# Retention and expert kernel: the block's output turned back by transposes, with the gate logits taken from the turned-over side in four column groups and added up over the heads by one product

## The chip, the cores and the metric

The kernel runs on one core of one Trainium2 chip. The metric is the device time of one execution in microseconds (us); of several executions the median is given. The profile is one execution on the same core, taken by the hardware profiler. Engines are named as in its rows: PE is TensorE's matmuls and PEld its weight loads, DVE is VectorE, ACT is ScalarE, POOL is GpSimd, SP is SyncE, which issues most transfers.

## The reference

A retention layer (attention with a decay per head, no softmax) over 4 batches of 768 tokens with 8 heads of 64, then a layer of 8 experts of which each token takes one:

```python
gamma = 1.0 - 2.0 ** (-5.0 - np.arange(H, dtype=np.float32))
scale = 1.0 / np.sqrt(D)
for t in range(S):
    state = gamma[None, :, None, None] * state + np.einsum('bhd,bhe->bhde', k[:, :, t], v[:, :, t])
    y[:, :, t] = scale * np.einsum('bhd,bhde->bhe', q[:, :, t], state)
...
x = np.ascontiguousarray(attn_out.transpose(0, 2, 1, 3)).reshape(B * S, H * D)
...
logits = x @ w_gate + modality_bias[modality_id]
e_idx = np.argmax(logits, axis=1)
...
h = np.maximum(x[mask] @ w1[e], 0.0)
out[mask] = gate_w[mask, None] * (h @ w2[e])
```

There are 3072 tokens; `x` has 512 columns, an expert's inner layer 1024. `gate_w` is the softmax probability of the chosen expert. All is float32.

## The kernel before, in words

**Retention** goes through 24 blocks of 128 tokens, six to a batch. Of each block the kernel computes masked scores (PE, then DVE writes `a`, L212 in later blocks and L283 in earlier ones), the running state (`st`) and the block's output turned over, `yT`: features on the partitions, tokens along the row, four groups of 128 features, each group two heads. The decay is pulled apart: keys and values are scaled beforehand by a power that falls with the token's place, and the outputs have to be multiplied by `gain`, a number for each token and head. Blocks 0 to 8 are computed whole (`whole_scores`, `whole_state`, `whole_out`), blocks 9 to 23 in quarters, so that two small products run side by side in the array.

**`tokens_out(n, yT)`** (L367 to L406) makes rows of tokens out of `yT`. `wgt` holds for each of the four feature groups an identity of 128 columns (copied by DVE at L146) and beside it the gate's weights of that group's two heads, 16 columns. One product with `yT` as stationary operand and `wgt` as moving operand gives 144 columns: the group's features turned back, and the logits that each head adds, before the gain. Two groups go to one PSUM bank, two to another (`x_0`, `x_1`; four products, eight records, L375). DVE multiplies the logits of a bank by the gain (`lh`, L383), and the features of the first bank too (`xs`, L383); ScalarE does the features of the second bank, a head at a time (`xs`, four ACTIVATE, L397); at the end DVE adds up `lh` over the heads into `lg` (L404). The rows `xs` are later scattered to a table in DRAM, from which the experts fetch them; `lg` of three blocks goes through a routing step (softmax, choice, ranks, lists) in small pieces on all engines.

**Experts** work in jobs of 256 tokens. Weights come as `raw` by SP's queue; ScalarE takes the rounded part `hi_e` (L780), DVE the rest `lo_e` (L782); rows fetched are turned over by PE (`xp_e`, L825); first layer `h_e` (L840) and second layer `o_e` (L855) are products in three terms (hi hi, hi lo, lo hi). Late in the kernel the last tokens are done in units of 32 (`uh_u`, L909, a product in four column groups).

**Order.** The order on PE, ACT, DVE and SP is that in which the program's text issues the instructions (`tc.manual_schedule`). The retention is a generator. At first it runs alone, with the first expert weights fetched beside it; from about 67 us on it is mixed with the expert jobs: a job yields after each feature group, every third of its steps takes one step of the retention, every second one calls `tick()`, which takes the next routing piece from the list `todo`. `tokens_out` of a block is called after the step in which the next block's scores are masked. Thus between a block's `x` on PE and its `lh` on DVE there may stand masked scores, cuts of weights or routing pieces in DVE's queue, while PE has expert products behind `x` in its own.

## Time and profile before

| | |
|---|---|
| median of 3 runs | 431.44 us (429.03 to 433.25) |
| the profiled execution's own time | 433.4 us |
| its span, first to last instruction | 431.5 us, mean granted clock 0.978 |
| busy: PE, PEld | 403.3, 353.1 us |
| busy: DVE, ACT, POOL | 249.4, 207.6, 103.9 us |
| transfers | 92.79 MB, 215 GB/s in the mean |
| PE `x` (L375) | 192 records, 31.8 us, 24 blocks |
| DVE `lh` (L383), 128x32 | 48 instructions, 184 ns each |
| DVE `xs` (L383), 128x256 | 24 instructions, 414 ns each |
| DVE sum into `lg` (L404) | 24 instructions, 272 ns each |
| ACT `xs` (L397), 128x64 | 96 instructions, 315 ns each |

A row of the profile's groups gives line, engine, operation, the tile written and those read, the shapes, how many, then busy us and the mean of one in ns, then the idle time of the engine just before and what ended it. A row of the timeline gives start and duration in us, then engine, line, operation and tiles; in brackets the idle time before it and what ended that. A stretch is a window of time, with each engine's busy time in it, the clock granted to TensorE (1.00 is full), the share of time in which transfers ran, and GB/s. A row of the chain of waits gives start, duration and group; the chain is followed back from the last instruction. L12 is line 12 of the kernel.

### The profile page before, as it was taken

The page shows a single profiled execution, that of the slowest core. Times are in us where ns is not written, and L with a number is a line of the kernel's source. Part 1 is how long each engine was busy: PE and PEld are TensorE (multiplying, and loading weights), DVE is VectorE, ACT ScalarE, POOL GpSimd, SP SyncE. Part 2 cuts the span into 40 slices and gives each one's busy share as a digit, 9 for nine tenths or more (in the row PEclk, how much of TensorE's full clock was granted, in tenths as well). Part 3 has the DMA queues.
Part 4 walks back from the last instruction along what each step waited for, and adds up shares of the span by engine and source line. Part 5 has one row for each costly group of instructions (what it writes and reads, how often), then busy time and mean ns, then how long its engine had stood idle before and what let it go on. Part 6 is the DMA issues. An engine that isn't in the chain of part 4 may idle for free.

```text
span 431.5 us, 12024 instructions
## 1 busy us (share of the span) xinstructions
PE 403.3 (93%) x4596; PEld 353.1 (82%) x4596; DVE 249.4 (58%) x590; ACT 207.6 (48%) x420; POOL 103.9 (24%) x130
## 2 busy tenths in 40 slices
PE   4987979899999999999999999999999999999990
PEld 3876869888988977988888988979898998869850
DVE  1766547856636666646945765967564655635400
ACT  1324245635546455546545646636464646535310
POOL 2425301413052123113500401210774101001010
PEclk9999688999999999999999999999999999999997
DMA  8999746967796954237840304842264989995000
GB/s 287 388 402 333 306 165 235 356 203 238 238 349 244 323 212 154 88 103 235 281 162 27 139 21 160 254 162 75 94 226 125 367 286 350 352 394 219 2 25 20
DMA packets 30891, 92.79 MB, mean 215 GB/s; under 512 B 5550, under 2 KB 5678, under 8 KB 30832
## 3 DMA queue, kind: packets, MB, share of 16 engines
q1 hardware_dynamic: 25360, 77.83, 52.0%
q0 software_dynamic: 5184, 13.67, 8.7%
q8 instruction: 37, 0.61, 0.6%
q10 hardware_dynamic: 288, 0.50, 0.4%
q14 instruction: 22, 0.18, 0.1%
HBM read 94.84 MB, written 17.21 MB: 260 GB/s over the span
## 4 chain that ended last, share of the span: by engine, by line
PE 66%; issue 8%; DMA 5%; DVE 3%; ACT 2%; POOL 1%; POOLq 0%; SPq 0%; ACTq 0%
PE o_e L855 25%; PE h_e L840 23%; PE x L375 4%; PE st L267 3%; PE h_s L840 3%; PE sc L267 3%; PE y L267 2%; DMA wa_u<-in_w_dram 2%; PE xp_e L825 2%; DMA wb_u<-in_w_dram 2%; DMA kv<-in_qkv_dram 1%; DVE lo_e L782 1%; ACT hi_e L780 1%; ACT xs L397 1%; POOL out_dram L868 1%
## 5 line engine op out<-in xcount | busy, mean ns | idle before, releaser
L782 DVE TENSOR_TENSOR lo_e<-raw,hi_e 128x1024 fp32r<-128x1024 f32 x80 | 100.0, 1250 | 76.5 <-ACT hi_e L780 68.6
L840 PE MATMUL h_e<-xTh,hi_e 128*128 128x256 f32 x320 | 92.0, 287 | 0.0
L840 PE MATMUL h_e<-xTl,hi_e 128*128 128x256 f32 x320 | 90.3, 282 | 0.0
L840 PE MATMUL h_e<-xTh,lo_e 128*128 128x256 f32 x320 | 90.3, 282 | 0.0
L780 ACT CAST hi_e<-raw 128x1024 fp32r<-128x1024 f32 x80 | 83.8, 1049 | 2.8 <-DMA raw<-in_w_dram 2.8
L855 PE MATMUL o_e<-hi_e,hTh 128*128 128x512 f32 x160 | 66.1, 413 | 0.0
L855 PE MATMUL o_e<-lo_e,hTh 128*128 128x512 f32 x160 | 63.1, 395 | 0.0
L855 PE MATMUL o_e<-hi_e,hTl 128*128 128x512 f32 x160 | 63.1, 394 | 0.0
L840 PEld LDWEIGHTS h_e<-xTh,hi_e 128*128 128x128 f32 x320 | 60.9, 190 | 0.7
L840 PEld LDWEIGHTS h_e<-xTh,lo_e 128*128 128x128 f32 x320 | 60.7, 190 | 0.3
L840 PEld LDWEIGHTS h_e<-xTl,hi_e 128*128 128x128 f32 x320 | 60.8, 190 | 0.0
L868 POOL DMA_INDIRECT out_dram<-o_e,xg_e x20 | 21.5, 1073 | 109.7 <-ACT o_e L867 89.5
L789 ACT ACTIVATE hTh<-h_e 128x256 fp32r<-128x256 f32 x80 | 30.7, 388 | 33.7 <-PE h_e L840 29.9
L1024 POOL TENSOR_TENSOR vd<-kv,cst 128x512 f32<-128x512 f32 x24 | 26.5, 1103 | 74.7 <-DMA kv<-in_qkv_dram 29.9
L397 ACT ACTIVATE xs<-x,cst 128x64 f32<-128x64 f32 x96 | 22.3, 315 | 45.2 <-DVE lh L383 20.4
L481 POOL DMA_INDIRECT x_dram<-xs,pos x24 | 27.6, 1152 | 65.4 <-DVE a L212 29.8
L790 DVE SCALAR_TENSOR_TENSOR hTl<-h_e,hTh 128x256 fp32r<-128x256 f32 x80 | 33.0, 419 | 16.0 <-ACT hTh L789 14.4
L855 PEld LDWEIGHTS o_e<-lo_e,hTh 128*128 128x128 f32 x160 | 30.1, 188 | 7.1
L855 PEld LDWEIGHTS o_e<-hi_e,hTh 128*128 128x128 f32 x160 | 30.1, 188 | 6.2
L855 PEld LDWEIGHTS o_e<-hi_e,hTl 128*128 128x128 f32 x160 | 30.2, 189 | 5.6
L262 ACT COPY s<-st 128x256 f32<-128x256 f32 x36 | 13.6, 378 | 40.4 <-PE y L267 16.1
L867 ACT ACTIVATE o_e<-o_e,xg_e 128x512 f32<-128x512 f32 x20 | 13.8, 690 | 39.6 <-issue 24.0
(193 smaller groups left out, 696.0 us busy)
## 6 DMA issues: line engine op xcount, KB each, us to landing
raw<-in_w_dram SPq DMA_DIRECT2D x104, 512.0 KB
kv<-in_qkv_dram SPq DMA_DIRECT2D x24, 512.0 KB
kq<-in_qkv_dram SPq DMA_DIRECT2D x23, 512.0 KB
xg_e<-x_dram SPq DMA_DIRECT2D x20, 257.0 KB
wa_u<-in_w_dram SPq DMA_DIRECT2D x8, 512.0 KB
wb_u<-in_w_dram SPq DMA_DIRECT2D x16, 256.0 KB
xg_s<-x_dram SPq DMA_DIRECT2D x4, 257.0 KB
x_dram<-xs,pos POOLq DMA_INDIRECT x24
```

The source lines that it names most:

```text
L267: nc.tensor.matmul(out_, l, r, start=start, stop=True, skip_group_check=True)
L375: nc.tensor.matmul(px[:, g], yT[:, 2 * u + g], wgt[:, 2 * u + g], start=(g == 0), stop=(g == 1), skip_group_check=True,)
L397: nc.scalar.activation(x[:, i], px[:, i // 2, rows(i % 2)], AF.Copy, scale=gain[:, c, 4 * u + i : 4 * u + i + 1],)
L481: ins = nc.gpsimd.indirect_dma_start(out=x_dram[:, :], out_offset=bass.IndirectOffsetOnAxis(ap=pos[:, i : i + 1], axis=0), in_=xs, in_offs ...
L780: nc.scalar.copy(hi, raws[m][i])
L782: nc.vector.tensor_tensor(lo, raws[m][i], hi.bitcast(F32), op=ALU.subtract)
L789: nc.scalar.activation(hi, src, AF.Relu)
L790: nc.vector.scalar_tensor_tensor(lo, src, 0.0, hi.bitcast(F32), op0=ALU.max, op1=ALU.subtract)
L840: nc.tensor.matmul(ph, s["w1"][f // 2][wi][:, o : o + P], s["xT"][kc // 2][a][:, kc % 2, :], start=(n == 0), stop=(n == 3 * KC - 1),)
L855: nc.tensor.matmul(po, hT[f][a][:, hh * P : (hh + 1) * P], s["w2"][f // 2][wi][:, (f % 2) * DM : (f % 2 + 1) * DM], start=(n == 0), stop=( ...
L868: ins = nc.gpsimd.indirect_dma_start(out=out[:, :], out_offset=bass.IndirectOffsetOnAxis(ap=xg.bitcast(I32)[:, DM : DM + 1], axis=0), in_= ...
L1024: ins = nc.gpsimd.tensor_tensor(vds[n], vv, by[:, n % NCH].unsqueeze(2).to_broadcast([P, H, D]), op=ALU.mult)
```

## The change

`wgt` loses the identity: it holds, for each feature group, 32 columns of gate weights (16 of them used, the others zero), and comes by one transfer. The constants grow by 142 columns (`gainl`, `stepl`, `suml`).

`tokens_out` works in five steps. Into columns 256 to 383 of bank `xa` go four products with the gate's weights as stationary operand (32 columns) and `yT` as moving operand, each to its own 32 partitions: the logits turned over, group and head on the partitions, tokens along the row (L386). DVE multiplies them by `stepl` (the decay of the block, one number for each partition) and `gainl` (that of the token in the block) in one instruction into `lT` (L391). PE turns `yT` back by four transposes, two into columns 0 to 255 of `xa`, two into bank `xb` (L396). One product with `lT` as stationary operand and `suml`, ones at the right places, as moving operand adds up over the heads and turns the logits to tokens on partitions, into columns 384 to 391 of `xa` (L403); DVE copies them into `lg` (L404). The features are multiplied by the gain as before, DVE from `xa` (L411), ScalarE from `xb` (L417).

Up to block 7 the sum is issued right after the transposes; from block 8 on it is put into the list `sums`, and the next `tick()` issues it ahead of a routing piece.

```diff
ZROW = NE * NT
 
 ROW = DM + 2
-XW = P + 2 * NE
+LW = 32
 KC = DM // P
 FC = DF // P
 QW = KC * 256
 
-C_ID, C_MASK, C_DEC, C_IOTA, C_OUT, C_HALF, C_DECW, C_END = 0, 128, 256, 304, 312, 360, 424, 472
+C_ID, C_MASK, C_DEC, C_IOTA, C_OUT, C_HALF, C_DECW = 0, 128, 256, 304, 312, 360, 424
+C_GAINL, C_STEPL, C_SUML, C_END = 472, 600, 606, 614
 
 
 @with_exitstack
...
         nc.sync.dma_start(t, qkv[n][:, 2:4])
 
     cst = cp.tile([P, C_END], F32, name="cst")
-    wgt = cp.tile([P, NG, XW], F32, name="wgt")
+    wgt = cp.tile([P, NG, LW], F32, name="wgt")
     load_kq(0, 2)
     load_kv(0)
     nc.scalar.dma_start(cst, consts)
...
     gain = cst[:, C_OUT : C_OUT + NCH * H].rearrange("p (c h) -> p c h", h=H)
     half = cst[:, C_HALF : C_HALF + D]
     decw = cst[:, C_DECW : C_DECW + NCH * H].rearrange("p (c h) -> p c h", h=H)
+    gainl = cst[:, C_GAINL : C_GAINL + P]
+    stepl = cst[:, C_STEPL : C_STEPL + NCH]
+    suml = cst[:, C_SUML : C_SUML + NE]
 
     tbias = cp.tile([P, NN, NE], F32, name="tbias")
     iota3 = cp.tile([P, GRP, NE], F32, name="iota3")
...
         return modi
 
     def setup_a():
-        nc.vector.tensor_copy(wgt[:, :, :P], ident.unsqueeze(1).to_broadcast([P, NG, P]))
         nc.vector.memset(ones, 1.0)
         nc.vector.memset(cnt[0], 0.0)
 
...
         nc.scalar.copy(yT, py)
         return yT
 
+    sums = []
     def tokens_out(n, yT):
         xs = xrows[n] = wk.tile([P, ROW], F32, tag="xs", name=f"xs_{n}", bufs=6)
-        lh = wk.tile([P, H, NE], F32, tag="lh", name=f"lh_{n}")
         c = n % NCH
-        for u in range(2):
-            px = bank(f"x_{n}_{u}")[:, : 2 * XW].rearrange("p (b e) -> p b e", b=2)
-            for g in range(2):
-                nc.tensor.matmul(
-                    px[:, g], yT[:, 2 * u + g], wgt[:, 2 * u + g], start=(g == 0), stop=(g == 1),
-                    skip_group_check=True,
-                )
-            hs = slice(4 * u, 4 * u + 4)
-
-            def gained(out_, src, w):
-                shape = [P, 2, 2, w]
-                nc.vector.tensor_tensor(
-                    out_.rearrange("p (b j) w -> p b j w", b=2),
-                    src.rearrange("p b (j w) -> p b j w", j=2),
-                    gain[:, c, hs].rearrange("p (b j) -> p b j", b=2).unsqueeze(3)
-                    .to_broadcast(shape),
-                    op=ALU.mult,
-                )
-
-            gained(lh[:, hs], px[:, :, P:], NE)
-            x = xs[:, u * 2 * P : (u + 1) * 2 * P].rearrange("p (h d) -> p h d", h=4)
-            if u == 0:
-                gained(x, px[:, :, :P], D)
-            else:
-                for i in range(4):
-                    nc.scalar.activation(
-                        x[:, i], px[:, i // 2, rows(i % 2)], AF.Copy,
-                        scale=gain[:, c, 4 * u + i : 4 * u + i + 1],
-                    )
+        pa, pb = bank(f"xa_{n}"), bank(f"xb_{n}")
+        pl = pa[:, 2 * P : 3 * P]
+        for b in range(NG):
+            nc.tensor.matmul(
+                pl[b * LW : (b + 1) * LW], wgt[:, b], yT[:, b], start=True, stop=True,
+                skip_group_check=True,
+            )
+        lT = wk.tile([P, P], F32, tag="lT", name=f"lT_{n}", bufs=1)
+        nc.vector.scalar_tensor_tensor(
+            lT, pl, stepl[:, c : c + 1], gainl, op0=ALU.mult, op1=ALU.mult
+        )
+        for b in range(NG):
+            px = (pa, pb)[b // 2][:, b % 2 * P : (b % 2 + 1) * P]
+            nc.tensor.transpose(px, yT[:, b], ident)
         gr = n // GRP
         if n % GRP == 0:
             lg[gr] = sm.tile([P, GRP, NE], F32, tag="lg", name=f"lg_{gr}")
-        nc.vector.tensor_reduce(
-            lg[gr][:, n % GRP], lh.rearrange("p h e -> p e h"), axis=AX.X, op=ALU.add
-        )
+        def add_up():
+            pg = pa[:, 3 * P : 3 * P + NE]
+            nc.tensor.matmul(pg, lT, suml, start=True, stop=True, skip_group_check=True)
+            nc.vector.tensor_copy(lg[gr][:, n % GRP], pg)
+        if n + 1 < WHOLE:
+            add_up()
+        else:
+            sums.append(add_up)
+        nc.vector.tensor_tensor(
+            xs[:, : 2 * P].rearrange("p (h d) -> p h d", h=4),
+            pa[:, : 2 * P].rearrange("p (h d) -> p h d", h=4),
+            gain[:, c, :4].unsqueeze(2).to_broadcast([P, 4, D]), op=ALU.mult,
+        )
+        for i in range(4):
+            nc.scalar.activation(
+                xs[:, 2 * P + i * D : 2 * P + (i + 1) * D], pb[:, i * D : (i + 1) * D], AF.Copy,
+                scale=gain[:, c, 4 + i : 5 + i],
+            )
 
     shp = [P, GRP, NE]
     mid = {}
...
     todo = []
 
     def tick():
+        while sums:
+            sums.pop(0)()
         if todo:
             todo.pop(0)()
 
...
     def everything():
         load_kq(1)
         load_kv(1)
-        nc.sync.dma_start(wgt[:, :, P:], wgate)
+        nc.sync.dma_start(wgt, wgate)
         load_kq(2)
         load_kv(2)
         modi = load_small()
...
     dec = (gam[None, :] ** (-t[:, None])).reshape(NCH, 2, D, NG, 2).transpose(4, 2, 0, 1, 3)
     cst[:, C_DEC : C_DEC + NCH * H] = dec.reshape(P, NCH * H)
     dec = (gam[None, heads] ** (-t[:, None])).reshape(NCH, P, H)
-    cst[:, C_DECW:] = dec.transpose(1, 0, 2).reshape(P, NCH * H)
+    cst[:, C_DECW : C_DECW + NCH * H] = dec.transpose(1, 0, 2).reshape(P, NCH * H)
     cst[:, C_IOTA : C_IOTA + NE] = np.arange(NE)
 
     head = np.array([[2 * b + 1 - p // D for p in range(P)] for b in range(NG)])
...
     gain = gain.reshape(NCH, P, H)[:, :, head[:, ::D].reshape(H)]
     cst[:, C_OUT : C_OUT + NCH * H] = gain.transpose(1, 0, 2).reshape(P, NCH * H)
     cst[:, C_HALF : C_HALF + D] = np.tile(np.triu(np.ones((D, D))), (2, 1))
+    gl, sl, ul = np.zeros((NG, LW, P)), np.zeros((NG, LW, NCH)), np.zeros((NG, LW, NE))
+    for b in range(NG):
+        for j in range(2):
+            g, w = gam[head[b, j * D]], slice(j * NE, (j + 1) * NE)
+            gl[b, w] = g ** t[:P] / np.sqrt(D)
+            sl[b, w] = g ** (np.arange(NCH, dtype=np.float64) * P)
+            ul[b, w] = np.eye(NE)
+    cst[:, C_GAINL:C_STEPL] = gl.reshape(P, P)
+    cst[:, C_STEPL:C_SUML] = sl.reshape(P, NCH)
+    cst[:, C_SUML:] = ul.reshape(P, NE)
     ci = np.arange(NCAND)
     cand = np.zeros((NCAND, 4), f)
     cand[:, 0] = (ci % SPE) * SLOT
...
 
     mod = np.asarray(inputs["moe_modality_id"]).astype(np.int64).reshape(NN, P)
 
-    wg = np.zeros((2, D, NG, 2, NE), f)
+    wg = np.zeros((2, D, NG, LW // NE, NE), f)
     for j, w in enumerate(inputs["moe_w_gate"][order].reshape(NG, 2, D, NE).transpose(1, 2, 0, 3)):
         wg[j, :, :, j] = w
-    wg = wg.reshape(P, NG, 2 * NE)
+    wg = wg.reshape(P, NG, LW)
     mb = np.broadcast_to(inputs["moe_modality_bias"].reshape(1, 2, NE), (P, 2, NE))
     w1 = inputs["moe_w1"][:, order].reshape(NE, KC, P, 4, 256).transpose(0, 3, 2, 1, 4)
     w2 = inputs["moe_w2"].reshape(NE, 4, 2, P, DM).transpose(0, 1, 3, 2, 4)
```

On PE, around block 10 (`x` or `xa`/`xb` is the bank, 49 with an engine's name a semaphore counted by that engine), before:

```order
L267 MATMUL y_1448<-a_1332,vd_1063 64x64 x10
L375 MATMUL x_0_1552<-wgt,yT_1330 128x144 x2
L375 MATMUL x_1_1557<-wgt,yT_1330 128x144 x2
L855 MATMUL o_e_1482<-hi_e_1434,hTh_1409 128x512 [waits Activation_49]
L855 MATMUL o_e_1482<-hi_e_1434,hTl_1410 128x512
L855 MATMUL o_e_1482<-lo_e_1436,hTh_1409 128x512 [waits DVE_49]
```

and of the change:

```order
L274 MATMUL y_1487<-a_1367,vd_1094 64x64 x10
L386 MATMUL xa_1590<-yT_1365,wgt 32x128 x4
L396 MATMUL xa_1590<-cst,yT_1365 128x128 [waits DVE_49]
L396 MATMUL xa_1590<-cst,yT_1365 128x128
L396 MATMUL xb_1591<-cst,yT_1365 128x128 x2
L869 MATMUL o_e_1521<-hi_e_1473,hTh_1448 128x512 [waits Activation_49]
L869 MATMUL o_e_1521<-hi_e_1473,hTl_1449 128x512
L869 MATMUL o_e_1521<-lo_e_1475,hTh_1448 128x512
L869 MATMUL o_e_1521<-hi_e_1473,hTh_1469 128x512
L869 MATMUL o_e_1521<-hi_e_1473,hTl_1470 128x512
L869 MATMUL o_e_1521<-lo_e_1475,hTh_1469 128x512
L403 MATMUL xa_1590<-cst,lT_1596 128x8 [waits DVE_49]
```

Four products with no wait on DVE have become four logits products, a wait on DVE at the first transpose, four transposes, and, behind the job's next six products, the sum with a wait on DVE.

On DVE, the same block, before:

```order
L782 TENSOR_TENSOR lo_e_1505<-raw_102,hi_e_1503 128x1024 [waits DMAHW4_49,Activation_49]
L212 TENSOR_TENSOR a_1542<-sc_1449,cst 128x512 [waits PE_49]
L383 TENSOR_TENSOR lh_1551<-x_0_1552,cst 128x32 [waits PE_49]
L383 TENSOR_TENSOR xs_1550<-x_0_1552,cst 128x256 [waits DMASW4_49,Pool_49]
L383 TENSOR_TENSOR lh_1551<-x_1_1557,cst 128x32 [waits PE_49]
L404 TENSOR_REDUCE lg_1355<-lh_1551 128x8 [waits DVE_49]
```

and of the change:

```order
L796 TENSOR_TENSOR lo_e_1544<-raw_102,hi_e_1542 128x1024 [waits DMAHW4_49,Activation_49]
L219 TENSOR_TENSOR a_1581<-sc_1488,cst 128x512 [waits PE_49]
L391 SCALAR_TENSOR_TENSOR lT_1596<-xa_1590,cst 128x128 [waits PE_49]
L411 TENSOR_TENSOR xs_1589<-xa_1590,cst 128x256 [waits DMASW4_49,PE_49,Pool_49]
L796 TENSOR_TENSOR lo_e_1620<-raw_103,hi_e_1618 128x1024 [waits DMAHW5_49,Activation_49]
L404 COPY lg_1388<-xa_1590 128x8 [waits PE_49]
```

`lT` stands where the first `lh` stood, behind the same cut and the same masked scores; the copy into `lg` stands behind the next cut.

On DVE, around block 7 of the change:

```order
L219 TENSOR_TENSOR a_924<-sc_907,cst 128x512 [waits PE_49]
L796 TENSOR_TENSOR lo_e_939<-raw_102,hi_e_937 128x1024 [waits DMAHW0_49,Activation_49]
L391 SCALAR_TENSOR_TENSOR lT_948<-xa_942,cst 128x128 [waits PE_49]
L404 COPY lg_812<-xa_942 128x8 [waits PE_49]
L411 TENSOR_TENSOR xs_941<-xa_942,cst 128x256 [waits DMASW1_49,Pool_49]
L796 TENSOR_TENSOR lo_e_973<-raw_103,hi_e_971 128x1024 [waits DMAHW1_49,Activation_49]
```

Here a cut of expert weights, which waits for a transfer and for ScalarE, stands ahead of `lT`, and the sum's copy comes ahead of `xs`.

## The prediction

> **What bounds the kernel now.** I read the busy times first, then the stretches, then the chain of waits, and last the timeline of TensorE and VectorE around each block's `x` product, which is where the edit is.

> ```profile
> PE 403.3 (93%) x4596; PEld 353.1 (82%) x4596; DVE 249.4 (58%) x590; ACT 207.6 (48%) x420; POOL 103.9 (24%) x130
> ...
> 100.00:150.00 50.00, 49.98 (x724) 45.60 (x723) 28.87 (x63) 27.49 (x59) 12.36 (x16) 1.00 0.85 290
> 170.00:262.00 92.00, 91.29 (x1250) 81.86 (x1249) 57.06 (x142) 50.71 (x109) 18.64 (x27) 1.00 0.39 131
> ...
> 131.65 1.18 PE x L375 x8
> ```

> The first row is the page's busy time; the two after it are stretches (length, then busy PE, PEld, DVE, ACT, POOL, granted clock, DMA share, GB/s); the last is a step of the chain (start, us). From 100 us to the end of the retention blocks at 262 us TensorE has no gap: 49.98 of 50.00 and 91.29 of 92.00 at clock 1.00. It takes its instructions in program order, so there a microsecond of work or of waiting added to its queue is a microsecond of the whole, and one removed a microsecond won. Of the work in question each block costs 1.18 us of that chain: eight records of `x`, which wait for nothing. VectorE is busy 58%, but its queue is in order too, and what counts here is how late it comes to a block.

> **The new wait.** Before, `x` needs only `yT`; VectorE reads it later, and TensorE goes on with expert work at once. Afterwards the logits go into columns 256 to 383 of the same bank whose columns 0 to 255 take the first two transposes, and the first transpose carries a wait on VectorE in all 24 blocks. A wait for the bank's former user would stand on the bank's first writer, the logits product; so this one is for `lT`, the only VectorE reader in between. TensorE thus stops, after the logits, until VectorE has finished everything queued ahead of `lT`, and `lT`. What is queued behind on TensorE (the transposes, the expert products of the block, everything) stops with it.

> How long that is can be read off the kernel before: `lh` stands where `lT` will stand. The four late blocks (9, 14, 18, 21):

> ```profile
> 77.91 1.25 PE L375 MATMUL x<-wgt,yT 128*128 128x144 f32 x8
> 80.97 0.18 DVE L383 TENSOR_TENSOR lh<-x,cst 128x32 f32<-128x32 f32 x1
> ...
> 145.08 1.25 PE L375 MATMUL x<-wgt,yT 128*128 128x144 f32 x8
> 147.95 0.17 DVE L383 TENSOR_TENSOR lh<-x,cst 128x32 f32<-128x32 f32 x1
> ...
> 198.44 1.25 PE L375 MATMUL x<-wgt,yT 128*128 128x144 f32 x8
> 201.36 0.17 DVE L383 TENSOR_TENSOR lh<-x,cst 128x32 f32<-128x32 f32 x1
> ...
> 240.65 1.25 PE L375 MATMUL x<-wgt,yT 128*128 128x144 f32 x8
> 243.43 0.18 DVE L383 TENSOR_TENSOR lh<-x,cst 128x32 f32<-128x32 f32 x1
> ```

> From `x`'s start to `lh`'s start: 3.06, 2.87, 2.92, 2.78 us, together 11.63. Six blocks lie between (8, 11, 12, 13, 16, 17; the first and the last below), and six are met at once (10, 15, 19, 20, 22, 23; one below):

> ```profile
> 65.34 2.24 PE L375 MATMUL x<-wgt,yT 128*128 128x144 f32 x8
> 66.70 0.19 DVE L383 TENSOR_TENSOR lh<-x,cst 128x32 f32<-128x32 f32 x1 [1.26 <-PE x L375]
> ...
> 185.61 1.25 PE L375 MATMUL x<-wgt,yT 128*128 128x144 f32 x8
> 186.65 0.18 DVE L383 TENSOR_TENSOR lh<-x,cst 128x32 f32<-128x32 f32 x1
> ...
> 213.89 1.25 PE L375 MATMUL x<-wgt,yT 128*128 128x144 f32 x8
> 214.69 0.19 DVE L383 TENSOR_TENSOR lh<-x,cst 128x32 f32<-128x32 f32 x1
> ```

> The six between take 1.36, 1.37, 1.62, 1.08, 1.34 and 1.04, 7.81 in all; in the last kind `lh` starts 0.80 behind, that is, as soon as the first bank is full.

> **Costs, part by part.** Nothing in the trace has these shapes; the nearest rows (groups, timeline, chain):

> ```profile
> L639 DVE TENSOR_SCALAR gt<-pk,key 96x96 f32<-96x96 f32 x6 | 1.8, 304 | 0.0
> L790 DVE SCALAR_TENSOR_TENSOR hTl<-h_e,hTh 128x256 fp32r<-128x256 f32 x80 | 33.0, 419 | 16.0 <-ACT hTh L789 14.4 <-issue 1.6
> ...
> 43.64 0.21 DVE L610 COPY crep<-cnt 128x96 bf16<-128x96 bf16 x1
> 43.90 0.24 PE L615 MATMUL pc<-ones,crep 128*96 128x1 bf16 x1 [2.37 <-DVE crep L610]
> ...
> 128.29 0.87 PE xp_e L825 x8
> ...
> 373.02 1.86 PE uh_u L909 x32
> ```

> Removed: 1.18 us of `x` per block. Added on the path:
> - logits: four 32-column groups at 128 columns. `uh_u` does 16 such products of 256 columns in 1.86, so 0.465 for four; at 128 columns between half of it (0.23) and all of it, and I take 0.33. Where VectorE is free, `lT` then starts 0.45 to 0.79 behind the logits' start, taken as 0.55 with the hand-over; where VectorE is late, the logits lie inside the delay and cost nothing more.
> - `lT`: 304 ns (96x96) is the floor, 419 (128x256) the ceiling; a 128x128 lies at the floor, 0.30.
> - the way back: `crep` ends at 43.85, TensorE starts at 43.90: 0.05.
> - four transposes: `xp_e`'s eight take 0.87, 0.109 each, so 0.44; with the pipe just emptied up to 0.54. I take 0.50.
> - the sum: two records at 0.109 (each loads 128 columns of weights and streams 8), 0.22; in blocks 8 to 23 put off until VectorE has passed `xs`, so without a wait, except in block 8, where nothing of TensorE lies between: `xs` and the hand-over, 0.6.

> So a block gains d + 0.30 + 0.05 + 0.50 + 0.22 - 1.18 = d - 0.1, d being the delay. Blocks 8 to 23: 11.63 + 7.81 + 6 x 0.55 = 22.7, less 1.6, plus 0.6: **+21.7**.

> [...]

> Blocks 0 to 7 have gaps on TensorE, but the waits stand in the middle of dense pieces:

> ```profile
> 14.59 1.25 PE L375 MATMUL x<-wgt,yT 128*128 128x144 f32 x8
> 16.47 0.18 DVE L383 TENSOR_TENSOR lh<-x,cst 128x32 f32<-128x32 f32 x1
> ...
> 18.95 1.25 PE L375 MATMUL x<-wgt,yT 128*128 128x144 f32 x8
> 19.05 1.29 DVE L283 TENSOR_TENSOR a<-sc,cst 128x512 f32<-128x512 f32 x2 [1.01 <-PE sc L277]
> 20.26 0.18 DVE L383 TENSOR_TENSOR lh<-x,cst 128x32 f32<-128x32 f32 x1
> ...
> 30.02 1.23 PE L375 MATMUL x<-wgt,yT 128*128 128x144 f32 x8
> 31.91 0.17 DVE L383 TENSOR_TENSOR lh<-x,cst 128x32 f32<-128x32 f32 x1
> ```

> VectorE is at two masked scores (1.29) when `x` starts: 1.88 in block 0, 1.31 in 1, the same taken for 2 and 4, 1.89 in 3: 7.7, less 0.5, is +7.2. Blocks 5 and 6 are met at once: 2 x 0.45 = +0.9. The sum stands at once here and may wait for nothing, since `lT` is done. Block 7 is its own case, because `lT` stands behind a cut of expert weights that is itself late:

> ```profile
> 53.99 1.25 PE L375 MATMUL x<-wgt,yT 128*128 128x144 f32 x8
> 55.17 0.62 PE L267 MATMUL st<-vd,kv 64*64 64x64 f32 x13
> 57.25 0.33 PE L825 MATMUL xp_e<-cst,xg_e 128*128 128x128 f32 x1
> 58.41 1.23 DVE L782 TENSOR_TENSOR lo_e<-raw,hi_e 128x1024 fp32r<-128x1024 f32 x1 [4.22 <-ACT hi_e L780]
> 61.49 0.37 PE L267 MATMUL st<-vd,kv 64*64 64x64 f32 x2 [1.84 <-ACT s L262]
> ```

> `lo_e` ends at 59.64 whatever TensorE does, `lT` at 59.94; transposes and sum until 60.7; then the state and `y` products that ran 55.17 to 57.25, 2.1 us, to 62.8, and `xp_e` (0.87) to 63.7, where the chain stood at 61.49 before: about +2.3. Below, zero bounds it, if the gap that ended at 61.49 swallows the whole; above, the 4.6 from 55.2 to 59.9.

> Costed at nothing: the freed `lh`, the reduction and the second wait of ScalarE's `xs` (ScalarE is 48% busy; were its `xs` late, only a table of tokens would be), the removed copy of the identity, and the constants' larger load, whose landing is hidden by the first keys and queries.

> Sum: 21.7 + 7.2 + 0.9 + 2.3 = **+32.1** on the profiled 433.4, that is 465.5; that execution is 2.0 above the median of 431.44, so I forecast **464**.

> **Rivals.**

> *The clock falls (477).* Four stalls leave TensorE idle about 2.75 us (3 us of delay and `lT`, less the logits).

> ```profile
> 40.00:50.00 10.00, 7.63 (x74) 6.59 (x70) 7.76 (x31) 1.97 (x8) 3.54 (x4) 0.68 1.00 322
> 47.90 2.18 PE L375 MATMUL x<-wgt,yT 128*128 128x144 f32 x8
> ```

> After the 2.37 us idle that ended at 43.90 the stretch had a granted clock of 0.68, and `x` took 2.18 in place of 1.25: some 3 us lost. Four times that is +13, in all 477. Against it: one example only, and in a thinner stretch than those four have around them. [...]

> *VectorE has caught up (450).* While TensorE stands, VectorE is given no new scores, and it is busy 58%; the delays may shrink to the short kind everywhere. Then blocks 8 to 23 give 16 x 0.45 = 7.2 and 0.6, the early ones keep 7.2 + 0.9 + 2.3 = 10.4: +18.2, 451.6 on the profiled one, 450 by the median. For it: the share. Against it: the late blocks are late because routing steps, cuts and scores stand ahead of `lh` in VectorE's fixed order, and they still do.

> *The wait is met before it is reached (427).* If VectorE came to `lT` while the logits still stream, TensorE would stop nowhere: 0.33 + 0.44 + 0.22 = 0.99 in place of 1.18, -0.19 a block, 24 times -4.6, so 428.8 on the profiled execution and 427 by the median. It decides from a round trip below 0.2 us; even the blocks met at once have `lh` 0.80 behind `x`, and `lT` alone is 0.30.

> **How the numbers follow.** The forecast has 0.53 (its own range 453 to 474, from the bounds of `lT`, transposes, logits and block 7, and half of the long delays kept or not), the clock 0.22, VectorE caught up 0.18, the wait met 0.07. The range goes from 446 to 482 and takes in the first three. About 1% is what a measurement of this kernel can tell from no change; only the last case comes near it, 0.03 faster by more and 0.04 within. Slower: 0.93.

> **What would show it.** In the chain of waits of the changed kernel, TensorE's transposes (L396) waiting for VectorE's `lT` (L391) some 24 times, about 30 us in all, the longest in blocks 7, 9, 14, 18 and 21, with TensorE's busy time some 3 us lower and the stretch of 100 to 262 us no longer dense. `lT` at 0.30, the four transposes at 0.5, the sum at 0.2 and without a wait from block 9 on show the sizes. A granted clock below 1.00 behind the long stalls would show the first rival; waits under 1 us everywhere the second; no such row in the waits, the third, and the prediction wrong.

## The result and the profile after

The changed kernel takes 472.26 us (median of 6 runs, 470.49 to 473.82), the kernel before 431.47 (429.03 to 433.25): ratio 1.0933, 95% interval 1.0901 to 1.0966. That is 40.8 us slower, where 32.6 were forecast (464, range 446 to 482).

First the busy times, then TensorE's waits (line, what it waited for, us in total, times, longest), of the changed kernel:

```profile
PE 413.8 (88%) x4740; PEld 358.1 (76%) x4740; DVE 246.6 (52%) x565; ACT 210.8 (45%) x420; POOL 101.3 (21%) x130
...
PE xa L396 <- DVE lT L391: 34.6, 24, 3.5
PE sc L284 <- DMA kq<-in_qkv_dram: 5.3, 1, 5.3
PE pc L629 <- DVE crep L624: 2.4, 1, 2.4
```

The first row of the waits is new: in all 24 blocks the first transpose waits for VectorE's `lT`, 34.6 us together. TensorE's share falls from 93 to 88%. Yet its busy time grows by 10 us, though the work hardly does; the stalls filled, below, show that this is the clock.

Where the time went is best seen by cutting both executions at the same places of the program: the first block's `x` (now the logits), block 8's, block 23's, the end. First before, then after (stretch, length, then busy PE, PEld, DVE, ACT, POOL, granted clock, DMA share, GB/s):

```profile
14.59:65.34 50.75, 43.14 (x716) 37.19 (x714) 31.06 (x114) 18.45 (x63) 15.95 (x21) 0.89 0.87 313
65.34:258.21 192.87, 189.33 (x2711) 169.18 (x2708) 122.67 (x302) 103.81 (x220) 45.43 (x57) 0.99 0.59 200
258.21:431.50 173.29, 162.41 (x1081) 139.15 (x1079) 90.76 (x163) 82.55 (x132) 37.52 (x35) 0.98 0.56 194
```

```profile
15.68:75.29 59.61, 44.62 (x764) 37.60 (x762) 29.92 (x102) 20.16 (x63) 15.99 (x21) 0.86 0.72 255
75.29:295.61 220.32, 197.21 (x2807) 173.26 (x2805) 121.00 (x287) 105.34 (x220) 42.49 (x57) 0.95 0.52 177
295.61:471.90 176.29, 162.72 (x1086) 138.91 (x1086) 90.42 (x162) 82.48 (x132) 37.79 (x35) 0.98 0.54 191
```

Of the 40.4 us between the two spans 1.1 come ahead of block 0's `x`, 8.9 in blocks 0 to 7, 27.5 in blocks 8 to 22, 3.0 behind (from block 23 on). In the long middle stretch TensorE's idle time went from 3.5 to 23.1 us, and its busy time from 189.3 to 197.2 at a clock of 0.95 in place of 0.99. The idle time afterwards is the waits for `lT`, 22.8 us, and one of 0.35 for the sum of block 8; the 3.5 us that TensorE was idle there before are no longer seen.

A block that VectorE meets at once (10), and a late one (18), in the timeline of the changed kernel:

```profile
105.84 0.43 PE L386 MATMUL xa<-yT,wgt 128*32 128x128 f32 x8
106.33 0.35 DVE L391 SCALAR_TENSOR_TENSOR lT<-xa,cst 128x128 f32<-128x128 f32 x1 [2.41 <-PE xa L386]
106.74 0.44 PE L396 MATMUL xa<-cst,yT 128*128 128x128 f32 x2 [0.47 <-DVE lT L391]
107.01 0.38 PE L396 MATMUL xb<-cst,yT 128*128 128x128 f32 x2
107.15 0.47 PE L869 MATMUL o_e<-hi_e,hTh 128*128 128x512 f32 x1
...
220.53 0.43 PE L386 MATMUL xa<-yT,wgt 128*32 128x128 f32 x8
221.05 1.87 DVE L796 TENSOR_TENSOR lo_e<-raw,hi_e 128x1024 fp32r<-128x1024 f32 x1
222.84 0.68 DVE L219 TENSOR_TENSOR a<-sc,cst 128x512 f32<-128x512 f32 x1
223.45 0.33 DVE L391 SCALAR_TENSOR_TENSOR lT<-xa,cst 128x128 f32<-128x128 f32 x1
223.83 0.69 PE L396 MATMUL xa<-cst,yT 128*128 128x128 f32 x2 [2.88 <-DVE lT L391]
```

In block 10 VectorE stands ready (it had waited 2.41 us), and the way there and back still costs 0.47. In block 18 a cut (`lo_e`) and the masked scores are ahead of `lT`, and TensorE stands 2.88 us. Its first transposes afterwards take 0.69 where block 10's take 0.44: they run at half clock (0.51 granted from 223 to 230 us, last section).

### The profile page after: what moved, and what is told of

The parts are those of the page before. It is cut to its first block, busy times and chain, and to the rows that moved or that the text cites. A ratio compares the mean times of both kernels' runs of the same rounds, so it can differ in the third digit from the quotient of the medians.

```text
span 471.9 us, 12279 instructions
## 1 busy us (share of the span) xinstructions
PE 413.8 (88%) x4740; PEld 358.1 (76%) x4740; DVE 246.6 (52%) x565; ACT 210.8 (45%) x420; POOL 101.3 (21%) x130
## 5 line engine op out<-in xcount | busy, mean ns | idle before, releaser
L854 PE MATMUL h_e<-xTh,hi_e 128*128 128x256 f32 x320 | 95.0, 297 | 0.0
L854 PE MATMUL h_e<-xTh,lo_e 128*128 128x256 f32 x320 | 92.6, 290 | 0.0
L854 PE MATMUL h_e<-xTl,hi_e 128*128 128x256 f32 x320 | 92.4, 289 | 0.0
L854 PEld LDWEIGHTS h_e<-xTh,hi_e 128*128 128x128 f32 x320 | 63.3, 198 | 0.7
L854 PEld LDWEIGHTS h_e<-xTh,lo_e 128*128 128x128 f32 x320 | 63.2, 198 | 0.3
L854 PEld LDWEIGHTS h_e<-xTl,hi_e 128*128 128x128 f32 x320 | 63.2, 197 | 0.0
L417 ACT ACTIVATE xs<-xb,cst 128x64 f32<-128x64 f32 x96 | 22.2, 314 | 56.3 <-issue 25.8
L396 PE MATMUL xa<-cst,yT 128*128 128x128 f32 x48 | 12.0, 337 | 34.6 <-DVE lT L391 34.6
L495 POOL DMA_INDIRECT x_dram<-xs,pos x24 | 25.9, 1078 | 65.7 <-DVE xs L461 23.3
L396 PEld LDWEIGHTS xa<-cst,yT 128*128 128x128 f32 x48 | 5.4, 156 | 41.2 <-DVE lT L391 41.2
```

What stands on the lines that cost most here:

```text
L396: nc.tensor.transpose(px, yT[:, b], ident)
L417: nc.scalar.activation(xs[:, 2 * P + i * D : 2 * P + (i + 1) * D], pb[:, i * D : (i + 1) * D], AF.Copy, scale=gain[:, c, 4 + i : 5 + i],)
L495: ins = nc.gpsimd.indirect_dma_start(out=x_dram[:, :], out_offset=bass.IndirectOffsetOnAxis(ap=pos[:, i : i + 1], axis=0), in_=xs, in_offs ...
L854: nc.tensor.matmul(ph, s["w1"][f // 2][wi][:, o : o + P], s["xT"][kc // 2][a][:, kc % 2, :], start=(n == 0), stop=(n == 3 * KC - 1),)
```

## The experiments

Theory A is that of the prediction: TensorE stands because the transposes share a bank with what `lT` reads. Theory B is that the change costs by its own work (transposes, weight loads, the sum). Theory C is the first rival: part of the loss is the clock. The ratio behind each median, with its 95% interval, is to the kernel before, run beside it; it is taken from the runs and not from the two medians, so that it differs a little from their quotient.

**The transposes first** (same banks, logits behind them):

```diff
         pl = pa[:, 2 * P : 3 * P]
+        for b in range(NG):
+            px = (pa, pb)[b // 2][:, b % 2 * P : (b % 2 + 1) * P]
+            nc.tensor.transpose(px, yT[:, b], ident)
...
-        for b in range(NG):
-            px = (pa, pb)[b // 2][:, b % 2 * P : (b % 2 + 1) * P]
-            nc.tensor.transpose(px, yT[:, b], ident)
         gr = n // GRP
```

> The transposes are issued ahead of the logits product, in the same two banks; lT, the sum and everything else as in the change. The first transpose then waits for no lT; only the sum does (at once in blocks 0 to 7, put off from block 8 on). Theory A (the shared bank makes TensorE wait for lT; the waits of blocks 8 to 23 are 23 us of the 34.6, and the half clock after the long ones is theirs too): 472 less 23, less some 4 where the transposes now fill part of the early waits, less 6 to 12 of clock: 433 to 439, TensorE's waits for lT at 7 to 8 us in all. Theory A without the clock: about 445. Theory B (what is paid is the work itself, eight transposing records, weight loads and the sum in each block): 468 or more.

Measured: 445.89 us, 1.0297 (1.0246 to 1.0349), 26 us less than the change. B falls; A is borne out in kind, though the time lies 7 us above A's range. It meets the figure given for A without a share of the clock (about 445), but not for that reason: between block 8 and block 23 this kernel has a granted clock of 0.99, where the change has 0.95. What A left out is in the profile: its waits, and block 10.

```profile
PE xa L403 <- DVE lT L394: 8.0, 8, 2.9
...
PE xa L403 <- DVE xs L411: 3.6, 4, 1.6
```

```profile
100.09 0.44 PE L387 MATMUL xa<-cst,yT 128*128 128x128 f32 x2
100.37 0.38 PE L387 MATMUL xb<-cst,yT 128*128 128x128 f32 x2
100.68 0.43 PE L389 MATMUL xa<-yT,wgt 128*32 128x128 f32 x8
101.03 0.50 PE L869 MATMUL o_e<-hi_e,hTh 128*128 128x512 f32 x1
```

The sum still waits for `lT` (8.0 us), in four blocks for `xs`, which reads the same bank (3.6 us), and the block costs 0.94 us from its first transpose to the next product. The next kernel does the same work in 0.77.

**A bank of its own** for logits and sum, the order as in the change:

```diff
-        pl = pa[:, 2 * P : 3 * P]
+        pc = bank(f"xl_{n}")
+        pl = pc[:, 2 * P : 3 * P]
...
-            pg = pa[:, 3 * P : 3 * P + NE]
+            pg = pc[:, 3 * P : 3 * P + NE]
```

> The order of the change is kept, but logits and sum get a third bank of their own. Theory A: as with the transposes first, 433 to 439, since the transposes no longer share a bank with what lT reads. Theory B: 468 or more. A rival to A: a third bank per block makes other products wait for a free bank, some 0.3 to 0.6 us in each of 16 blocks, so 440 to 450.

Measured: 439.92 us, 1.0168 (1.0125 to 1.0212): 32.3 of the 40.8 us gone by a change of bank alone. The time lies between A's range (up to 439) and that of the rival, a lack of banks (from 440); the profile decides. Its waits, the same stretches, and block 10:

```profile
PE xl L404 <- DVE lT L392: 9.8, 9, 2.3
```

```profile
14.53:72.37 57.84, 46.52 (x764) 38.12 (x762) 31.18 (x109) 20.20 (x63) 15.96 (x21) 0.85 0.78 271
72.37:262.23 189.86, 187.59 (x2803) 164.62 (x2797) 120.40 (x287) 105.36 (x220) 46.30 (x57) 1.00 0.61 206
262.23:438.70 176.47, 162.98 (x1087) 139.05 (x1086) 90.46 (x162) 82.50 (x132) 37.81 (x35) 0.98 0.55 191
```

```profile
97.67 0.43 PE L387 MATMUL xl<-yT,wgt 128*32 128x128 f32 x8
98.03 0.44 PE L397 MATMUL xa<-cst,yT 128*128 128x128 f32 x2
98.30 0.38 PE L397 MATMUL xb<-cst,yT 128*128 128x128 f32 x2
98.44 0.47 PE L870 MATMUL o_e<-hi_e,hTh 128*128 128x512 f32 x1
...
99.91 0.28 PE L404 MATMUL xl<-cst,lT 128*128 128x8 f32 x2
100.05 0.48 PE L870 MATMUL o_e<-hi_e,hTh 128*128 128x512 f32 x1
```

The middle stretch is 189.9 us, 3.0 shorter than before. Up to 1.2 of them are work: a block's logits, transposes and sum cost 0.77 and 0.14, against 0.99 from `x` at 213.89 to the next product at 214.88 in the kernel before. Another 1.3 are idle time (3.5 before, 2.3 here), and part of the rest is the clock: before, the first 2.1 us of this stretch ran at half clock. No lack of banks shows: of the 2.3 us idle here 2.2 are waits of the sum for `lT`. What is left is in the stretch of blocks 0 to 7, 7.1 us longer than before, where the sum waits at once, and behind block 23, 3.2 longer.

**`lT` computed twice** (nothing else changed):

```diff
+        for _ in range(2):
             nc.vector.scalar_tensor_tensor(
                 lT, pl, stepl[:, c : c + 1], gainl, op0=ALU.mult, op1=ALU.mult
             )
```

> VectorE computes lT twice in a row in every block, 0.34 us each. Theory A: the wait grows by 0.34 in each of 24 blocks, 8.2 us, and block 14's wait of 2.08 grows to 2.42, where it may cost clock as well: 480 to 484. Theory B (VectorE is off the path, only TensorE's work counts): 472.

Measured: 484.03 us (median of three of its four runs; the fourth took 490.53 at a clock of 0.934), 1.1164 (1.1092 to 1.1235), 11.8 more than the change and at the upper end of A's range.

```profile
PE xa L397 <- DVE lT L392: 44.4, 24, 3.9
```

The waits grew by 9.8, 0.41 a block, for 0.34 of VectorE's work: time added on VectorE ahead of the transposes is TensorE's in full. That is A's slope, not B's zero. The spans of the two profiled executions differ by 12.2 us; the other 2.4 are TensorE's busy time (416.2 in place of 413.8, for the same work at a mean clock of 0.944 in place of 0.950).

**The stalls filled** with needless transposes, so that TensorE isn't idle in the long ones:

```diff
+        if n in (7, 9, 14, 18, 19, 21):
+            for i in range(16):
+                nc.tensor.transpose(pb[:, 2 * P : 3 * P], yT[:, i % NG], ident)
```

> In blocks 7, 9, 14, 18, 19 and 21, whose waits are the longest (2.08 to 3.46 us), TensorE does 16 needless transposes (about 1.75 us) into a free part of bank xb between logits and transposes, so that it is not idle. Theory C (about 12 us of the loss are the half clock that follows those waits): 458 to 462, clock 1.00 from block 8 on. Without a share of the clock: 472, and a little more where the filling outlasts the wait.

Measured: 461.57 us, 1.0693 (1.0620 to 1.0765), 10.7 less than the change with more work to do.

```profile
15.03:74.83 59.80, 44.35 (x779) 37.41 (x778) 30.54 (x106) 20.19 (x63) 16.03 (x21) 0.91 0.72 259
74.83:285.67 210.84, 197.20 (x2883) 173.12 (x2877) 120.92 (x287) 105.35 (x220) 43.16 (x57) 1.00 0.54 185
285.67:460.30 174.63, 162.84 (x1087) 139.04 (x1086) 90.45 (x162) 82.50 (x132) 37.80 (x35) 0.98 0.54 192
```

The middle stretch is 9.5 shorter than in the change, at clock 1.00 in place of 0.95; the transposes start when `lT` allows it, as before (in block 18 `lT` starts 2.92 behind the logits in both). Theory C holds, beside A: of the 27.5 us lost there, 9.5 are clock and 18.0 remain. The own bank takes 21.0 more from this stretch, those 18.0 and the 3.0 by which it is then shorter than before. What else is gained here is not clock: the stretch of blocks 0 to 7 is as long as in the change (59.8 against 59.6), and behind block 23 the 1.7 us are a wait for rows of tokens, 0.4 in place of 2.0.

**The sums later.** The bank of its own, and the sum one tick more behind in the blocks that still waited:

```diff
-        if n + 1 < WHOLE:
+        if n in (2, 5):
             add_up()
         else:
-            sums.append(add_up)
+            sums.append([2 if n in (0, 1, 3, 4, 6, 7, 9, 18) else 1, add_up])
...
-        while sums:
-            sums.pop(0)()
+        for left in sums:
+            left[0] -= 1
+        while sums and sums[0][0] <= 0:
+            sums.pop(0)[1]()
```

> As with the bank of its own, and the sum put off by one more tick in blocks 0, 1, 3, 4, 6, 7, 9 and 18, so that it stands behind the next block's products or the next expert products (blocks 2 and 5 keep it at once, since routing reads it there). Theory A (waits and clock are all of the loss; the work itself is a block's 0.77 us of logits and transposes and 0.14 us of sum against 0.99 us of x, as the rows with the own bank show): 9 us of waits for lT go, the work wins 24 x 0.08 = 2: 428 to 432 where before has 431.5, with waits for lT below 2 us in all. Rival (the change also costs something outside these waits, a later table of tokens or a lack of banks): 434 to 438.

Measured: 431.35 us, 0.9982 (0.9966 to 0.9997) against 432.19.

```profile
PE xl L404 <- DVE lT L392: 5.3, 4, 3.6
...
PE pc L629 <- DVE crep L624: 2.9, 2, 2.4
PE xp_e L839 <- DMA xg_e<-x_dram: 1.4, 1, 1.4
```

```profile
64.76:253.56 188.80, 187.29 (x2805) 164.59 (x2798) 121.62 (x287) 105.36 (x220) 46.58 (x58) 1.00 0.61 208
253.56:428.70 175.14, 162.76 (x1087) 139.03 (x1086) 90.42 (x162) 82.50 (x132) 37.81 (x35) 0.98 0.55 192
```

The whole loss is gone. Two things fall short of A's expectation: 5.3 us of waits are left, 3.6 of them in block 7; and though the middle stretch is 4.1 us shorter than before, the span is only 2.8 shorter, since the stretch behind is 1.9 longer: there TensorE waits 1.4 us for rows of tokens. What sets their landing was not tried. Part of the gain is the clock and not the change's work: before, the middle stretch began with 2.1 us at half clock, and the stretch of blocks 0 to 7 had a clock of 0.89 (50.8 us) where this kernel has 0.97 (50.3 us). By the medians the gain is 0.8; the two profiled executions stand 2.0 above (before) and 0.8 below (this one) theirs.

**The kernel before, with its own idle time filled**, a test of C where nothing of the change is present:

```diff
         pc = bank(f"pc{t}")
+        if t == min(EVENTS):
+            for _ in range(14):
+                nc.tensor.transpose(pc[:, P : 2 * P], ident, ident)
```

> The kernel before, with 14 needless transposes of the identity (about 1.9 us) on TensorE ahead of the product pc of the second routing group only, where TensorE sits idle for 2.37 us and the clock halves afterwards. If the halving comes from TensorE's own idleness in a window of 3.4 us, the 6.8 us at half clock behind it are gone, and about 3 us are won: 428 to 429.5. If it has another cause: 431.5 as before.

Measured: 431.22 us, 0.9978 (0.9964 to 0.9992). The half clock behind that gap is gone, as C says, but only 1.0 us of the 3 came through, so that the time alone would speak for the other cause. First the kernel before, then this one:

```profile
40.00:60.00 20.00, 16.19 (x237) 13.81 (x233) 10.91 (x41) 5.43 (x17) 5.08 (x5) 0.83 0.70 221
...
PE pt L688 <- DVE ohs L678: 2.1, 2, 1.5
...
PE xp_e L825 <- DMA xg_e<-x_dram: 1.1, 1, 1.1
```

```profile
40.00:60.00 20.00, 15.13 (x242) 13.08 (x241) 10.68 (x39) 5.03 (x15) 5.09 (x5) 0.96 0.66 210
...
PE pt L691 <- DVE ohs L681: 3.6, 3, 1.9
PE xp_e L828 <- DMA xg_e<-x_dram: 3.2, 2, 1.6
```

The clock of this stretch is 0.96 in place of 0.83. But TensorE now waits 3.2 us for the first rows, where it waited 1.1, and 3.6 at `pt`, where it waited 2.1: time won on TensorE there is in part spent waiting again.

**Block 7's sum later still**, aimed at the 3.6 us left:

```diff
-            sums.append([2 if n in (0, 1, 3, 4, 6, 7, 9, 18) else 1, add_up])
+            sums.append([3 if n == 7 else 2 if n in (0, 1, 3, 4, 6, 9, 18) else 1, add_up])
```

> As the late sums, with block 7's sum put off by one tick more, behind the first turned rows xp_e and the next block's state, because in the late sums TensorE stands 3.56 us at that sum, the longest wait left, and the clock halves behind it for 3.4 us. If that wait is what is left of the change's cost: xp_e (1 us at full clock) moves into it and half of 3.4 us of half clock goes, 428.5 to 430 where the late sums have 431.3. Rival (the start is paced by the landing of expert weights and rows, so that the wait only moves on to the state's copy on ScalarE or to the rows): 431, no change against the late sums.

Measured: 431.09 us, 0.9972 (0.9950 to 0.9994) against 432.82. The rival is right about the time: the wait only moved.

```profile
PE xp_e L839 <- DMA xg_e<-x_dram: 4.4, 3, 1.6
...
PE xl L404 <- DVE lT L392: 2.3, 3, 0.8
```

The waits for `lT` shrink from 5.3 to 2.3 us, those for rows grow from 1.4 to 4.4. Both versions with late sums thus stand 0.2 to 0.3% below the kernel before, short of the 1% that the prediction took as what a measurement of this kernel can tell from no change.

## Why the prediction was right, and where it was short

The mechanism is the one forecast, and it is shown: the wait of the first transpose for `lT`, 24 times. Forecast were some 24 waits of 30 us together; there are 24 of 34.6. Another bank alone takes back 32.3 us, and with it the transposes of block 10 follow the logits without a wait (98.03 behind 97.67). In one bank the wait stands on the first transpose although the columns are disjoint: it is in the program, as the order of PE shows. Whether the chip needs it there, no run shows: a run without the wait in one bank was not tried.

The number was nearer than its terms. The time lies between the forecast, 464, and the first rival, 477, and nearer to the rival; terms that were too low and too high offset each other. Between the two profiled executions, where 32.1 were forecast and 40.4 measured, term by term:
- *The delay is `lh`'s delay before.* From the logits' start to `lT`'s it held within half a microsecond in 13 of the 16 blocks from 8 to 23, and came to 23.7 us in all against 22.7 forecast. That the sum held is in part luck. Block 8 (0.50 in place of 1.36) is no late block: VectorE waited for `x` there, and `x` ran at half clock (2.24 us in place of 1.25). Block 14 (2.11 in place of 2.87) was earlier. Block 19, read as met at once, became long (2.87): its `lh` stood behind a cut and masked scores before, too, and only came in time because the cut began 0.96 us ahead of `x`. First the cut before, then the cut and `lT` of the change:

```profile
212.93 1.23 DVE L782 TENSOR_TENSOR lo_e<-raw,hi_e 128x1024 fp32r<-128x1024 f32 x1 [0.28 <-ACT hi_e L780]
...
240.66 1.97 DVE L796 TENSOR_TENSOR lo_e<-raw,hi_e 128x1024 fp32r<-128x1024 f32 x1 [0.28 <-ACT hi_e L794]
...
243.16 0.33 DVE L391 SCALAR_TENSOR_TENSOR lT<-xa,cst 128x128 f32<-128x128 f32 x1
```

  In the change the cut begins 0.37 behind the logits (240.29) and takes 1.97. The stalls are not the reason: with the late sums, where no transpose waits for `lT`, the delay in block 19 is 2.86 as well. What the reason is was not tried. In the other five blocks read as met at once VectorE was seen waiting for `x` (0.40 to 2.57 us), and there the delay stayed short.
- *The work.* Forecast 0.30 for `lT`, 0.50 for transposes (0.06 of it for an emptied pipe: in the kernel before, the first record of `xp_e` at 58.66 us, behind 1.09 us of idle time, stands 0.16 ahead of the second, where the records that follow stand 0.11 apart), 0.22 for the sum, against 1.18 of `x`: measured 0.34, 0.41, 0.14 (and 0.36 of logits), against 0.99 from `x`'s start to the next product. The step of 1.18 in the chain runs to the end of `x`'s last record, and the next product starts before that. Both sides were too high by about the same, so that the difference per block came out.
- *Blocks 8 to 22 without the clock*: forecast 21.7 (with block 23), measured 18.0, though the waits, 22.8, were no shorter than forecast. The stretch before was read as without a gap, from its parts of 100 to 150 and 170 to 262 us. From block 8 on it held 3.5 us of idle time, 1.46 of them at 85 us and 0.68 at 165, and 2.1 us at half clock; the change has neither there beside its own waits, and that takes back some 4.5 us (3.5, and half of 2.1).
- *Blocks 0 to 7*: forecast 10.4, measured 8.9. Block 6, read as met at once, waits 1.35 us: VectorE is at a routing piece there, as it was before, when `lh` came 1.76 behind `x`. (The upper bound for block 7, 4.6 "from 55.2 to 59.9", should be 4.7.)
- *The start*: forecast nothing, measured 1.1. About 0.3 is the larger load of constants, which is not hidden: POOL's first `vd` waits for it until 7.45 us in place of 7.16. The rest is the clock: it is first recorded as full at 14.9 us, before at 12.8, and 16 records of `st` ahead of block 0 take 1.07 in place of 0.63.
- *The stretch behind block 23*: forecast nothing, measured 3.0. Two of these are a wait for rows, which the kernels without the wait for `lT` in block 23 show too (1.9 with the transposes first, 2.4 with the bank of its own, 1.4 with the late sums), so that it isn't `lT`'s.
- *The clock*: this is the term that the sum lacked. The prediction put the half clock behind the long stalls among the rivals, at 0.22, and left it out of the sum. It is there: 9.5 us in the middle stretch, by the filled stalls. With it the sum would have been 41.6 in place of 32.1. TensorE's busy time, named as a sign and expected some 3 us lower, is 10.5 higher for the same reason. The row that spoke for it, 2.37 us of idle time with 0.68 granted afterwards, was right and was given too little weight: beside a wait of 3.46 us three of 2.77 to 2.88 us made the clock fall here.
- *VectorE has caught up* fell: eleven of the 24 waits are above 1.3 us. *The wait is met before it is reached* fell in the change. The own bank with late sums comes near it, with 431.35 and not 427: it waits elsewhere, and of the 4.1 us that its middle stretch wins 1.9 go in the stretch behind block 23.

## What to carry to other kernels

Before two products share a bank, ask who reads the first one: where TensorE is full, as here, the second then waits for the reader and for everything queued ahead of the reader (24 waits of 34.6 us together), and most of the price can be read before the change from how late that reader comes now. Here a bank of its own together with a sum put off behind other products cost nothing that could be measured; the bank alone still cost 8 us. Count the clock beside the stall where the granted clock falls after such stalls anywhere in the trace: the four stalls of 2.77 us and more in the middle stretch, 11.9 us together, cost some 9.5 us more. And expect part of a gain in one dense stretch to be given back where TensorE then waits for transfers (with the late sums 1.9 of 4.1 us, 1.4 of them a wait for rows).

## What the runs showed of the hardware

```profile
90.00:97.00 7.00, 5.54 (x27) 5.54 (x28) 3.15 (x10) 1.31 (x5) 4.45 (x4) 0.52 0.84 324
223.00:230.00 7.00, 6.17 (x18) 5.01 (x19) 1.21 (x3) 0.93 (x4) 0.00 (x0) 0.51 0.24 77
274.00:281.00 7.00, 5.82 (x28) 5.83 (x29) 2.73 (x8) 2.24 (x6) 3.72 (x7) 0.52 0.30 113
```

Seven microseconds at half clock each, two windows: in the first of them TensorE still waited for a part, so that only the second was full (busy 0.56, 0.78 and 0.73 in the first, 1.00 in the second).

The order of the same products matters as well: logits in 32-column groups ahead of the transposes cost 0.77 us in block 10 (the bank of its own), behind them 0.94 (the transposes first). The gap is between the last transposes and the product that follows (0.14 before an expert product, 0.31 before the logits). Why was not tried.
